# Fewer, larger transfers for wo and w2, an earlier last K, and later zero fills in a decode kernel bound by its loads

## Chip, cores, metric

One core of a Trainium2 chip (trn2). The metric is the device time of one execution in microseconds; a kernel is run several times and the median is given. Ratios are the mean time of one kernel's runs over that of the other's of the same rounds, so they are not quite the ratio of the medians quoted beside them. The limit for "faster" or "slower" is 2%, which is 10.5 us.

## The reference, cut to what matters

Four sequences, one new token each. Attention over the last 2048 positions of a K and V cache (32 heads of 192), its projection with wo, a gated FFN (w1, w3, w2) beside it, and the input added:

```python
B, D, Hq, Dh, Sk, F = 4, 640, 32, 192, 8192, 1536
xn = layernorm(x)                                       # (4, 1, 640) bfloat16
q = xn @ wq                                             # wq (640, 6144)
k, v = k_cache[:, :, Sk - 2048:], v_cache[:, :, Sk - 2048:]
p = softmax(einsum("bhqd,bhkd->bhqk", q, k) * Dh ** -0.5)
attn = einsum("bhqk,bhkd->bhqd", p, v).reshape(4, 1, 6144) @ wo   # wo (6144, 640)
ffn = (silu(xn @ w1) * (xn @ w3)) @ w2                  # w1, w3 (640, 1536), w2 (1536, 640)
return x + attn + ffn
```

K and V of one head are 3072 KB each, 64 such loads; all else together is 21.6 MB. Every byte is used once.

## The kernel before

One stream of loads is issued from the sync engine. A step of the schedule is a quarter of a head: VectorE multiplies K by the query (`mult`), TensorE adds over the head dimension (`adder`), VectorE finishes the scores; then softmax and the products with V (`pv`). Sums of several heads stand in one PSUM bank (`po`) and are scaled, transposed and projected together (`ge_turn`, `ge_proj`).

```python
HG, KBUFS, VBUFS = 4, 2, 3            # four heads per projection group; buffers for K and V
def wo_load(hg):                      # 8 loads, 7680 B in each partition
    wo_t = wopool.tile([P, RPP * D], BF16, tag="wo")                        # RPP = 6, two buffers
    nc.sync.dma_start(out=wo_t[:], in_=A_wo[hg * QW:(hg + 1) * QW, :].rearrange("(p i) n -> p (i n)", i=RPP))
...
qbc = ...                             # the queries, copied from PSUM by ScalarE and VectorE
for i in range(2):                    # zero fills, ahead of the first mult
    o_ps = ps_o.tile([P, 2 * Dh], FP32, tag="o_ps", name="o_ps")
    nc.vector.memset(o_ps[:], 0.0)
acc = ps_acc.tile([P, N0], FP32, name="acc"); nc.vector.memset(acc[:], 0.0)
...
def w1_load():                        # 512 rows, 64 rows as half rows; then the last 64 rows:
    we = wopool.tile([LF, 2 * F], BF16, tag="wo", name="w1e")
    nc.gpsimd.memset(we[:], 0.0); nc.gpsimd.memset(wt[0:LF, FH:], 0.0)
    ...
def w1_low(n):                        # four loads on three DMA engines ("e" is 3)
    nc.sync.dma_start(out=we[n * CT:n * CT + LP, :], in_=w[b0:b0 + 2 * LP, :].rearrange("(i e s) n -> e i (s n)", e=LE, s=2))
    ...
W2C = [0, FC - 8, FC - 4, FC - 1, FC] # w2 in four loads of 4, 4, 3 and 1 rows per partition
...
for h in range(H - 2, H):             # the end: V30, V31, w2, w2, wo, wo, w2, w2
    add(NU - 6, 0, load_v, h)
add(NU - 6, 0, w2_load, 0); add(NU - 6, 0, w2_load, 1)
add(NU - 6, 0, wo_load, NG - 2); add(NU - 6, 0, wo_load, NG - 1)
add(NU - 6, 0, w2_load, 2); add(NU - 6, 0, w2_load, 3)
```

## Time and profile before

| | before |
|---|---|
| time, median of the runs at hand for the prediction | 525.47 us (525.42 to 525.69) |
| span of the profiled execution | 523.7 us |
| bytes read; mean rate | 222.96 MB; 426 GB/s |
| busiest compute engine | PE, 69% of the span |
| DMA packets | 11904 |
| last packet of the load queue ends | 520.63 us |

In the lines of the profile PE is TensorE, PEld its weight loads, DVE VectorE, ACT ScalarE, POOL GpSimd and SPq the queue of the sync engine; "clock" is the share of the full TensorE clock that was granted.

The first thing to see is that all loads together would take 512.3 us on sixteen engines at 27.2 bytes per ns with no fixed cost at all. That leaves little to win anywhere but in the fixed cost of packets, in how evenly the engines are loaded, and in the first and last microseconds. The lines themselves are in the prediction.

### The profile page before, as it was taken

The numbers are of one execution on the slowest core, as the hardware profiler recorded it, in microseconds if no ns is written. First come the engines' busy times: TensorE is split into PE (matmuls) and PEld (weight loads), VectorE is DVE, ScalarE is ACT, GpSimd is POOL, SyncE is SP. The second block draws the span as 40 slices with busy tenths as digits, with TensorE's granted clock in tenths as the row PEclk, the third lists the DMA queues.
The fourth block names the chain that finished last, engine by engine and source line by source line (L and its number), as shares of the span: only waits on it lengthen the run. The fifth ranks groups of instructions, "written<-read, shape, count | busy, mean of one in ns | idle before, by whom it ended". The sixth has DMA issues, their size and how long they took to land.

```text
span 523.7 us, 4813 instructions
## 1 busy us (share of the span) xinstructions
PE 358.9 (69%) x2337; PEld 74.5 (14%) x1643; DVE 339.2 (65%) x410; ACT 57.3 (11%) x179; POOL 5.6 (1%) x12
## 2 busy tenths in 40 slices
PE   0976756887658776757557768576686876655785
PEld 0100111121111111111111111111111111111122
DVE  3248953687656767577647877467666867667671
ACT  2121111111001110110000111001101100001111
POOL 4000000000000000000000000000000000000000
PEclk9989986898788988799987988799878888999889
DMA  9999999999999999999999999999999999999996
GB/s 391 420 443 421 435 431 428 437 427 429 431 435 428 433 424 445 422 434 432 434 432 433 428 435 434 430 429 432 431 435 432 429 435 430 433 432 429 435 422 276
DMA packets 11904, 223.26 MB, mean 426 GB/s; under 512 B 1332, under 2 KB 1608, under 8 KB 3052
## 3 DMA queue, kind: packets, MB, share of 16 engines
q1 hardware_dynamic: 11868, 222.96, 99.3%
q8 instruction: 15, 0.25, 0.2%
q14 instruction: 5, 0.04, 0.0%
q10 hardware_dynamic: 16, 0.01, 0.0%
HBM read 222.96 MB, written 0.01 MB: 426 GB/s over the span
## 4 chain that ended last, share of the span: by engine, by line
DMA 60%; PE 19%; DVE 15%; ACT 3%; issue 2%; SPq 1%; DVEq 0%
DMA kt<-in_A_k_cache_dram 44%; PE ps L303 11%; DMA w<-in_B_w_dram 10%; DVE pr L292 10%; DMA vt<-in_A_v_cache_dram 5%; PE po L376 4%; DVE sc L311 2%; PE qps L258 2%; ACT ex L339 1%; DVE z L347 1%; DMA x_sb<-in_A_x_dram 1%; PE mt L333 1%; ACT L339 0%; ACT negm L336 0%; PE mt L320 0%
## 5 line engine op out<-in xcount | busy, mean ns | idle before, releaser
L303 PE MATMUL ps<-pr,idb 128*128 128x512 bf16 x768 | 217.3, 426 | 140.5 <-DVE pr L292 140.5
L292 DVE TENSOR_TENSOR pr<-kt,qbc 128x3072 bf16<-128x3072 bf16 x128 | 223.5, 1747 | 101.2 <-DMA kt<-in_A_k_cache_dram 101.2
L311 DVE TENSOR_REDUCE sc<-ps 128x16 f32<-128x512 f32 x128 | 87.1, 681 | 2.7 <-PE ps L303 2.7
L355 PE MATMUL o_ps<-vt,z 128*8 128x384 bf16 x1024 | 53.4, 345 | 0.2 <-DVE z L347 0.2
L376 PE MATMUL po<-o_sb,sel_w 128*32 128x192 f32 x128 | 49.2, 518 | 0.6 <-ACT o_sb L358 0.6
L347 DVE TENSOR_TENSOR z<-ex,mask_b 128x256 bf16<-128x256 bf16 x32 | 13.5, 423 | 41.3 <-ACT ex L339 41.3
L355 PEld LDWEIGHTS <-z 128*8 128x8 bf16 x1024 | 24.5, 89 | 95.2 <-issue 83.5
L358 ACT COPY o_sb<-o_ps 128x384 f32<-128x384 f32 x32 | 15.3, 479 | 189.6 <-PE o_ps L355 189.6
L328 ACT ACTIVATE gneg<-gmax 1x128 f32<-1x128 f32 x32 | 9.8, 308 | 164.6 <-DVE gmax L325 164.6
L320 PEld LDWEIGHTS mt<-idf,lmax 128*1 128x1 f32 x32 | 3.4, 105 | 132.1 <-issue 131.1
L376 PEld LDWEIGHTS po<-o_sb,sel_w 128*32 128x32 f32 x128 | 13.9, 131 | 30.0 <-issue 28.8
L303 PEld LDWEIGHTS <-idb 128*128 128x128 bf16 x124 | 12.0, 96 | 37.7 <-issue 31.6
L333 PEld LDWEIGHTS mt<-ones_ff,gneg 1*128 1x128 f32 x64 | 9.6, 186 | 47.9 <-issue 44.5
L258 PE MATMUL qps<-wt,xnT 128*128 128x512 bf16 x60 | 16.2, 438 | 0.0
L336 ACT COPY negm<-mt 128x1 f32<-128x1 f32 x32 | 5.1, 159 | 72.4 <-PE mt L333 72.4
L333 PE MATMUL mt<-ones_ff,gneg 1*128 1x1 f32 x64 | 12.3, 259 | 0.7 <-ACT gneg L328 0.7
L325 DVE TENSOR_REDUCE gmax<-mt 1x4 f32<-1x128 f32 x32 | 8.8, 275 | 6.0 <-PE mt L320 5.7
L363 PEld LDWEIGHTS po<-rsum,tot_w 128*32 128x32 f32 x64 | 4.4, 108 | 51.0 <-ACT ex L339 34.7
L320 PE MATMUL mt<-idf,lmax 128*1 128x128 f32 x32 | 11.3, 353 | 0.0
L339 ACT ACTIVATE ex<-sc,negm 128x64 bf16<-128x64 f32 x32 | 11.1, 348 | 1.0
L279 PE MATMUL acc<-wo_t,oT 128*4 128x320 bf16 x96 | 9.2, 298 | 1.3 <-DMA wo_t<-in_A_wo_dram 1.3
L214 PE MATMUL xnT_ps<-idb,xn 4*128 4x4 bf16 x5 | 0.4, 178 | 13.5 <-DVE xn L209 13.5
(74 smaller groups left out, 78.7 us busy)
## 6 DMA issues: line engine op xcount, KB each, us to landing
kt<-in_A_k_cache_dram SPq DMA_DIRECT2D x32, 3072.0 KB, 19.0
vt<-in_A_v_cache_dram SPq DMA_DIRECT2D x32, 3072.0 KB, 26.1
wo_t<-in_A_wo_dram SPq DMA_DIRECT2D x8, 960.0 KB, 20.8
wt<-in_A_wq_dram SPq DMA_DIRECT2D x2, 3072.0 KB
w<-in_B_w_dram SPq DMA_DIRECT2D x1, 1920.0 KB
wt<-in_A_wq_dram SPq DMA_DIRECT2D x1, 1536.0 KB, 19.5
w<-in_B_w_dram SPq DMA_DIRECT2D x1, 1536.0 KB
w<-in_B_w_dram SPq DMA_DIRECT2D x2, 640.0 KB
```

Of the source, the lines that this page charges most:

```text
L258: nc.tensor.matmul(qp[:], lhsT=xnT[:, kc].rearrange("p a b -> p (a b)"), rhs=wq_rows[kc][:, (c0 + i) * QC:(c0 + i + 1) * QC], start=(kc == ...
L292: nc.vector.tensor_tensor(out=pr[:], in0=kts[h][:, g * JQ:(g + 1) * JQ, :], in1=qbc[:, h * Dh:(h + 1) * Dh].unsqueeze(1).to_broadcast([P, ...
L303: nc.tensor.matmul(ps[:], lhsT=idb[:], rhs=pr[:, :, kk * DD:(kk + 1) * DD], start=(kk == 0), stop=(kk == NK - 1))
L311: nc.vector.tensor_reduce(out=scs[h][:, g * JQ:(g + 1) * JQ], in_=pss.pop(u)[:], axis=AX.X, op=ALU.add)
L320: nc.tensor.transpose(out=mt[0:1, 0:P], in_=chs[h][0][:], identity=idf[:])
L328: nc.scalar.activation(out=gneg[:], in_=gmax[:].unsqueeze(1).to_broadcast([1, PB, B]), func=ACTF.Copy, scale=-SCALE)
L333: nc.tensor.matmul(mt[:, P:P + 1], lhsT=gneg[:].rearrange("o p b -> o (p b)"), rhs=ones_ff[:], start=True, stop=True)
L339: nc.scalar.activation(out=ex[:], in_=scs.pop(h)[:], func=ACTF.Exp, bias=negm[:, 0:1], scale=SCALE, accum_out=rsum[:])
L347: nc.vector.tensor_tensor(out=z[:], in0=ex[:].unsqueeze(2).to_broadcast([P, NJ, B]), in1=mask_b[:].unsqueeze(1).to_broadcast([P, NJ, B]), ...
L355: nc.tensor.matmul(o_ps[c * CT:c * CT + 2 * B, :], lhsT=z[:, 2 * jj:2 * jj + 2, :], rhs=vt[:, 2 * jj:2 * jj + 2, :], start=(jj < 4), stop= ...
L358: nc.scalar.copy(out=o_sb[:], in_=o_ps[:])
L376: nc.tensor.matmul(po[sl, 0:Dh], lhsT=sel_w[:, par].rearrange("p a b -> p (a b)"), rhs=o_sb[:, par * Dh:(par + 1) * Dh].rearrange("p (r i) ...
```

## The change

Its intent: fewer and larger packets (wo by eight heads, w2 at once, w1's last rows in two loads, not four); the last K in ahead of the last three V, so that only V and weights are outstanding at the end; and the first K products no longer behind zero fills that wait for ScalarE. The core of the diff:

```diff
-    HG: int = 4,
+    HG: int = 8,
+    FG: int = 4,
-    wopool = ctx.enter_context(tc.tile_pool(name="wo", bufs=2))
+    wopool = ctx.enter_context(tc.tile_pool(name="wo", bufs=1))
     def load_k(h):
-        kt = kpool.tile([P, NJ, Dh], BF16, tag="kt")
+        kt = (kpool if h < H - 1 else vpool).tile(...)      # load_v: the other way round
...
+    acc = ps_acc.tile([P, N0], FP32, name="acc")            # now before x is there
+    nc.vector.memset(acc[:], 0.0)
...
-    for i in range(2):
-        o_ps = ...; nc.vector.memset(o_ps[:], 0.0)          # ahead of the first mult
+    add(5, 9, o_zero)                                       # the same fills in step 5
...
-        we = wopool.tile([LF, 2 * F], BF16, tag="wo", name="w1e")
-        nc.gpsimd.memset(we[:], 0.0)
-        nc.gpsimd.memset(wt[0:LF, FH:], 0.0)
+        we = wopool.tile([LF, LS, F], BF16, tag="wo", name="w1e")   # LS = 5
+        nc.gpsimd.memset(we[:], 0.0)
...
-    W2C = [0, FC - 8, FC - 4, FC - 1, FC]                   # four w2 loads
+        nc.sync.dma_start(out=wt[:].rearrange("p c n -> p (c n)"), in_=w2_v.rearrange("p c n -> p (c n)"))
-    ends = {H - 2: (NU - 1, NU), H - 1: (NU + 3, NU + 4)}
+    ends = {H - 3: (NU - 1, NU), H - 2: (NU + 2, NU + 3), H - 1: (NU + 4, NU + 5)}
+    early = {H - 1: (NU - 10, -1)}                          # the last K
...
+    WOC = [0, RPP - 5, RPP - 2, RPP]                        # last wo load: 7, 3 and 2 rows
     for h in range(H - 2, H):
         add(NU - 6, 0, load_v, h)
+    add(NU - 6, 0, w2_load)
+    for i0, i1 in zip(WOC, WOC[1:]):
+        add(NU - 6, 0, wo_load, NG - 1, i0, i1)
+        add(e, 6, ge_proj, NG - 1, i0, i1, True)
+    add(e - 1, 8, ffn_out)
```

More of the change, by code (lines that the diff above doesn't have):

```diff
@@ L101 @@
     CT = 32
+    HB = HG * CT // P
     QW = HG * Dh
     RPP = QW // P
+    RW = Dh // RPP
     NU = H * GQ
@@ L109 @@
     assert JQ * DD == 512 and JQ % 2 == 0 and 2 * Dh <= 512 and 2 * N0 == D and N0 <= 512
-    assert (H * Dh) % QC == 0 and NQ % 6 == 0 and QW % P == 0 and Dh == CT * RPP and P == HG * CT and F == HG * CT * FC
-    assert 2 * H * Dh <= NJ * Dh and KBUFS == 2 and VBUFS == 3
+    assert (H * Dh) % QC == 0 and NQ % 6 == 0 and QW % P == 0 and Dh == RW * RPP and CT == HB * RW and P == FG * CT and F == FG * CT * FC
+    assert 2 * H * Dh <= NJ * Dh and KBUFS == 2 and VBUFS == 3 and HB * (Dh + 1) <= 512 and H // HG > 1
     nc.at_finalize(keep_loaded_weights)
@@ L138, in load_k @@
     def load_k(h):
-        kt = kpool.tile([P, NJ, Dh], BF16, tag="kt")
+        kt = (kpool if h < H - 1 else vpool).tile([P, NJ, Dh], BF16, tag="kt" if h < H - 1 else "vt", name="kt")
         nc.sync.dma_start(out=kt[:].rearrange("q j d -> q (j d)"),
@@ L142, in load_k, with load_v, wo_load @@
         kts[h] = kt
-    def load_v(h, n=1):
-        vt = vpool.tile([P, NJ, Dh], BF16, tag="vt")
-        for j in range(0, NJ, NJ // n):
-            nc.sync.dma_start(out=vt[:, j:j + NJ // n].rearrange("q j d -> q (j d)"),
-                              in_=v_win[:, h].rearrange("b (p j) d -> p b j d", p=PB)[:, :, j:j + NJ // n].rearrange("p b j d -> p b (j d)"))
-        vts[h] = vt
-    def wo_load(hg):
-        wo_t = wopool.tile([P, RPP * D], BF16, tag="wo")
-        nc.sync.dma_start(out=wo_t[:], in_=A_wo[hg * QW:(hg + 1) * QW, :].rearrange("(p i) n -> p (i n)", i=RPP))
-        wos[hg] = wo_t
+    def load_v(h):
+        vt = (vpool if h < H - 1 else kpool).tile([P, NJ, Dh], BF16, tag="vt" if h < H - 1 else "kt", name="vt")
+        nc.sync.dma_start(out=vt[:].rearrange("q j d -> q (j d)"),
+                          in_=v_win[:, h].rearrange("b (p j) d -> p b (j d)", p=PB))
+        vts[h] = vt
+    def wo_load(hg, i0=0, i1=RPP):
+        if i0 == 0:
+            wos[hg] = wopool.tile([P, RPP * D], BF16, tag="wo", name="wo_t")
+        nc.sync.dma_start(out=wos[hg][:, i0 * D:i1 * D],
+                          in_=A_wo[hg * QW:(hg + 1) * QW, :].rearrange("(p i) n -> p i n", i=RPP)[:, i0:i1, :].rearrange("p i n -> p (i n)"))
     x_sb = const.tile([B, D], BF16, name="x_sb")
@@ L216 @@
     nc.vector.tensor_copy(out=xnT[:], in_=xnT_ps[:].unsqueeze(2).to_broadcast([P, KC, PB, B]))
-    KM, PH, LE, LI = KC - 1, P // 2, 3, 4
-    LP, LF, LB = LE * LI, CT + LE * LI, KM * P + PH
-    assert D - LB == 5 * LP + LI and F % LE == 0
+    KM, LE, LI, LS = KC - 1, 3, 4, 5
+    LP, LF = LE * LI, CT + LE * LI
+    PH = D - KM * P - LP * LS - LI
+    LB = KM * P + PH
+    assert PH == P // 2 and F % LE == 0
     xm = ppool.tile([B, 2, PH, 2], BF16, tag="pr", name="xm")
@@ L227 @@
         nc.vector.tensor_copy(out=xm[:, i, :, i], in_=xn[:, KM * P:LB])
-    xe = ppool.tile([B, 3 + LE, LF], BF16, tag="pr", name="xe")
+    xe = ppool.tile([B, LS + LE, LF], BF16, tag="pr", name="xe")
     nc.gpsimd.memset(xe[:], 0.0)
-    for g in range(2):
-        b0 = LB + g * 2 * LP
-        nc.vector.tensor_copy(out=xe[:, 0:2, g * CT:g * CT + LP].rearrange("b s (e i) -> b s e i", i=LI),
-                              in_=xn[:, b0:b0 + 2 * LP].rearrange("b (i e s) -> b s e i", e=LE, s=2))
-    nc.vector.tensor_copy(out=xe[:, 2, 0:LP].rearrange("b (e i) -> b e i", i=LI),
-                          in_=xn[:, LB + 4 * LP:LB + 5 * LP].rearrange("b (i e) -> b e i", e=LE))
+    nc.vector.tensor_copy(out=xe[:, 0:LS, CT:LF].rearrange("b s (e i) -> b s e i", i=LI),
+                          in_=xn[:, LB:LB + LS * LP].rearrange("b (i e s) -> b s e i", e=LE, s=LS))
     for e in range(LE):
-        nc.vector.tensor_copy(out=xe[:, 3 + e, CT + e * LI:CT + (e + 1) * LI], in_=xn[:, LB + 5 * LP:D])
-    NX = KM + 2
-    xw_ps = ps_t.tile([P, NX + 3 + LE, B], BF16, tag="t", name="xw_ps")
+        nc.vector.tensor_copy(out=xe[:, LS + e, e * LI:(e + 1) * LI], in_=xn[:, LB + LS * LP:D])
+    xw_ps = ps_t.tile([P, KM + 2 + LS + LE, B], BF16, tag="t", name="xw_ps")
     for kc in range(KM):
@@ L243, with weights @@
         nc.tensor.transpose(out=xw_ps[:, KM + i, :], in_=xm[:, i].rearrange("b r h -> b (r h)"), identity=idb[0:B, 0:B])
-    for i in range(3 + LE):
-        nc.tensor.transpose(out=xw_ps[0:LF, NX + i, :], in_=xe[:, i, :], identity=idb[0:B, 0:B])
-    xw = const.tile([P, NX, NREP, B], BF16, name="xw")
-    nc.vector.tensor_copy(out=xw[:], in_=xw_ps[:, 0:NX, :].unsqueeze(2).to_broadcast([P, NX, NREP, B]))
-    xl = const.tile([LF, 3 + LE, NREP, B], BF16, name="xl")
-    nc.vector.tensor_copy(out=xl[:], in_=xw_ps[0:LF, NX:, :].unsqueeze(2).to_broadcast([LF, 3 + LE, NREP, B]))
+    for i in range(LS + LE):
+        nc.tensor.transpose(out=xw_ps[0:LF, KM + 2 + i, :], in_=xe[:, i, :], identity=idb[0:B, 0:B])
+    def weights(name, p, c0, c1):
+        t = const.tile([p, c1 - c0, NREP, B], BF16, name=name)
+        nc.vector.tensor_copy(out=t[:], in_=xw_ps[0:p, c0:c1, :].unsqueeze(2).to_broadcast([p, c1 - c0, NREP, B]))
+        return t
+    xw = weights("xw", P, 0, KM)
+    xh = weights("xh", P, KM, KM + 2)
+    xl = weights("xl", LF, KM + 2, KM + 2 + LS + LE)
     qbc = const.tile([P, H * Dh], BF16, name="qbc")
@@ L269, with o_zero @@
     o_banks = []
-    for i in range(2):
-        o_ps = ps_o.tile([P, 2 * Dh], FP32, tag="o_ps", name="o_ps")
-        nc.vector.memset(o_ps[:], 0.0)
-        o_banks.append(o_ps)
-    acc = ps_acc.tile([P, N0], FP32, name="acc")
-    nc.vector.memset(acc[:], 0.0)
+    def o_zero():
+        for i in range(2):
+            o_ps = ps_o.tile([P, 2 * Dh], FP32, tag="o_ps", name="o_ps")
+            nc.vector.memset(o_ps[:], 0.0)
+            o_banks.append(o_ps)
     def acc_half(i, lhsT, rhs, first=False, last=False):
@@ L283, in acc_add @@
             acc_half(i, lhsT, rhs, last=last)
-    po = ps_po.tile([P, Dh + 1], FP32, name="po")
+    po = ps_po.tile([P, HB * (Dh + 1)], FP32, name="po")
+    po_v = po[:, 0:HB * Dh].rearrange("p (i x r) -> p i x r", x=HB, r=RW)
     def x_add(i):
@@ L361, in ge_tot @@
     def ge_tot(h):
-        sl = slice((h % HG) * CT, (h % HG + 1) * CT)
-        nc.tensor.matmul(po[sl, Dh:Dh + 1], lhsT=tot_w[:].rearrange("p a b -> p (a b)"), rhs=rsums.pop(h)[:],
-                         start=True, stop=True)
+        blk, x = (h % HG) // HB, h % HB
+        nc.tensor.matmul(po[blk * CT:(blk + 1) * CT, HB * Dh + x:HB * Dh + x + 1], lhsT=tot_w[:].rearrange("p a b -> p (a b)"),
+                         rhs=rsums.pop(h)[:], start=True, stop=True)
         chs.pop(h)
     def ge_rec(hg):
-        rt = small.tile([P, 1], FP32, tag="rt", bufs=2, name="rt")
@@ L369, in ge_rec @@
-        nc.vector.reciprocal(out=rt[:], in_=po[:, Dh:Dh + 1])
+        rt = small.tile([P, HB], FP32, tag="rt", bufs=2, name="rt")
+        nc.vector.reciprocal(out=rt[:], in_=po[:, HB * Dh:HB * (Dh + 1)])
         rts[hg] = rt
     def ge_sum(h):
-        sl = slice((h % HG) * CT, (h % HG + 1) * CT)
+        blk, x = (h % HG) // HB, h % HB
         o_sb = o_sbs.pop(h)
         for par in range(2):
-            nc.tensor.matmul(po[sl, 0:Dh], lhsT=sel_w[:, par].rearrange("p a b -> p (a b)"),
+            nc.tensor.matmul(po_v[blk * CT:(blk + 1) * CT, :, x, :], lhsT=sel_w[:, par].rearrange("p a b -> p (a b)"),
@@ L377, in ge_sum @@
                              rhs=o_sb[:, par * Dh:(par + 1) * Dh].rearrange("p (r i) -> p i r", i=RPP), start=(par == 0), stop=(par == 1))
     def ge_turn(hg):
-        og = small.tile([P, RPP, CT], BF16, tag="og", bufs=1, name="og")
-        nc.vector.tensor_scalar_mul(out=og[:].rearrange("p i r -> p (i r)"), in0=po[:, 0:Dh],
-                                    scalar1=rts.pop(hg)[:, 0:1])
+        og = small.tile([P, RPP, HB, RW], BF16, tag="og", bufs=1, name="og")
+        nc.vector.tensor_tensor(out=og[:], in0=po_v, in1=rts.pop(hg)[:].unsqueeze(1).unsqueeze(3).to_broadcast([P, RPP, HB, RW]),
+                                op=ALU.mult)
@@ L383, in ge_turn, with ge_proj @@
         oT = small.tile([P, RPP, CT], BF16, tag="oT", bufs=2, name="oT")
-        nc.vector.transpose(out=oT[:].rearrange("p i r -> p (i r)"), in_=og[:].rearrange("p i r -> p (i r)"))
+        nc.vector.transpose(out=oT[:].rearrange("p i r -> p (i r)"), in_=og[:].rearrange("p i x r -> p (i x r)"))
         oTs[hg] = oT
-    def ge_proj(hg, i0, i1):
+    def ge_proj(hg, i0, i1, last=False):
         oT, wo_t = oTs[hg], wos[hg]
         for i in range(i0, i1):
-            acc_add(oT[:, i, 0:B], wo_t[:, i * D:(i + 1) * D])
@@ L393 @@
-    FW = F // HG
+            acc_add(oT[:, i, 0:B], wo_t[:, i * D:(i + 1) * D], last=last and i == RPP - 1)
+    FW = F // FG
     sT = const.tile([P, FW], FP32, name="sT")
@@ L397 @@
     ffn = {}
-    FM, FH = KM * F, KM * F + F // 2
+    FM = KM * F
     def w1_load():
-        w = B_w1
-        wt = fpool.tile([P, FH + F], BF16, tag="w", name="w1")
-        we = wopool.tile([LF, 2 * F], BF16, tag="wo", name="w1e")
+        wt = fpool.tile([P, FM + F // 2], BF16, tag="w", name="w1")
+        we = wopool.tile([LF, LS, F], BF16, tag="wo", name="w1e")
         nc.gpsimd.memset(we[:], 0.0)
-        nc.gpsimd.memset(wt[0:LF, FH:], 0.0)
-        nc.sync.dma_start(out=wt[:, 0:FM], in_=w[0:KM * P, :].rearrange("(p kc) n -> p (kc n)", kc=KM))
-        nc.sync.dma_start(out=wt[:, FM:FH], in_=w[KM * P:LB, :].rearrange("r (h n) -> (r h) n", h=2))
+        nc.sync.dma_start(out=wt[:, 0:FM], in_=B_w1[0:KM * P, :].rearrange("(p kc) n -> p (kc n)", kc=KM))
+        nc.sync.dma_start(out=wt[:, FM:], in_=B_w1[KM * P:LB, :].rearrange("r (h n) -> (r h) n", h=2))
         ffn["w1"], ffn["w1e"] = wt, we
     def w1_low(n):
-        w, wt, we = B_w1, ffn["w1"], ffn["w1e"]
-        if n < 2:
-            b0 = LB + n * 2 * LP
-            nc.sync.dma_start(out=we[n * CT:n * CT + LP, :],
-                              in_=w[b0:b0 + 2 * LP, :].rearrange("(i e s) n -> e i (s n)", e=LE, s=2))
-        elif n == 2:
-            nc.sync.dma_start(out=wt[0:LP, FH:FH + F], in_=w[LB + 4 * LP:LB + 5 * LP, :].rearrange("(i e) n -> e i n", e=LE))
+        b0, we = LB + LS * LP, ffn["w1e"]
+        if n == 0:
+            nc.sync.dma_start(out=we[CT:LF].rearrange("p s n -> p (s n)"),
+                              in_=B_w1[LB:b0, :].rearrange("(i e s) n -> e i (s n)", e=LE, s=LS))
         else:
-            nc.sync.dma_start(out=wt[CT:LF, FH:FH + F // LE], in_=w[LB + 5 * LP:D, :].rearrange("i (e n) -> e i n", e=LE))
+            nc.sync.dma_start(out=we[0:LP, 0, 0:F // LE], in_=B_w1[b0:D, :].rearrange("i (e n) -> e i n", e=LE))
     def w1_in():
@@ L426, in mm @@
         def mm(w, lhsT, rhs, c0=0, start=False, stop=False):
-            nc.tensor.matmul(ps[w * CT:(w + 1) * CT, c0:c0 + rhs.shape[1]], lhsT=lhsT.rearrange("p a b -> p (a b)"), rhs=rhs,
-                             start=start, stop=stop)
+            nc.tensor.matmul(ps[w * CT:(w + 1) * CT, c0:c0 + rhs.shape[1]], lhsT=lhsT.rearrange("p a b -> p (a b)"), rhs=rhs, start=start, stop=stop)
         def main(kc):
-            for w in range(HG):
+            for w in range(FG):
                 mm(w, xw[:, kc], wt[:, kc * F + w * FW:kc * F + (w + 1) * FW], start=(kc == 0), stop=(kc == KM - 1))
         main(0)
-        for w in range(HG):
+        for w in range(FG):
             c0 = FM + (w % 2) * FW
-            mm(w, xw[:, KM + w // 2], wt[:, c0:c0 + FW])
-        for i in range(2):
-            for w in range(HG):
-                mm(w, xl[:, i], we[:, i * F + w * FW:i * F + (w + 1) * FW])
-        for w in range(HG):
-            mm(w, xl[:, 2], wt[0:LF, FH + w * FW:FH + (w + 1) * FW])
+            mm(w, xh[:, w // 2], wt[:, c0:c0 + FW])
+        for i in range(LS):
+            for w in range(FG):
+                mm(w, xl[:, i], we[:, i, w * FW:(w + 1) * FW])
         FE = F // LE
         for e in range(LE):
-            for w in range(HG):
+            for w in range(FG):
                 c0, c1 = max(e * FE, w * FW), min((e + 1) * FE, (w + 1) * FW)
                 if c0 < c1:
-                    mm(w, xl[:, 3 + e], wt[0:LF, FH + c0 - e * FE:FH + c1 - e * FE], c0 - w * FW)
+                    mm(w, xl[:, LS + e], we[:, 0, c0 - e * FE:c1 - e * FE], c0 - w * FW)
         for kc in range(1, KM):
@@ L459, in w3_in @@
         for kc in range(KC):
-            for w in range(HG):
+            for w in range(FG):
                 nc.tensor.matmul(ffn["ps"][w * CT:(w + 1) * CT, :], lhsT=xnT[:, kc].rearrange("p a b -> p (a b)")[:, 0:CT],
@@ L473, with w2_load, ffn_out @@
     w2_v = B_w2.rearrange("(p c) n -> p c n", c=FC)
-    W2C = [0, FC - 8, FC - 4, FC - 1, FC]
-    def w2_load(i):
-        if i == 0:
-            ffn["w2"] = fpool.tile([P, FC, D], BF16, tag="w", name="w2")
-        c0, c1 = W2C[i:i + 2]
-        nc.sync.dma_start(out=ffn["w2"][:, c0:c1, :].rearrange("p c n -> p (c n)"),
-                          in_=w2_v[:, c0:c1, :].rearrange("p c n -> p (c n)"))
-    def ffn_out(i):
-        for c in range(*W2C[i:i + 2]):
-            acc_add(hT[:, c, 0:B], ffn["w2"][:, c, :], last=(c == FC - 1))
+    def w2_load():
+        wt = fpool.tile([P, FC, D], BF16, tag="w", name="w2")
+        nc.sync.dma_start(out=wt[:].rearrange("p c n -> p (c n)"), in_=w2_v.rearrange("p c n -> p (c n)"))
+        ffn["w2"] = wt
+    def ffn_out():
+        for c in range(FC):
+            acc_add(hT[:, c, 0:B], ffn["w2"][:, c, :])
     sched = defaultdict(list)
@@ L497 @@
         if h >= KBUFS:
-            add((h - KBUFS + 1) * GQ, 0, load_k, h)
+            add(*early.get(h, ((h - KBUFS + 1) * GQ, 0)), load_k, h)
         if h < H - 2:
@@ L518 @@
     e = ends[H - 1][1] + 1
-    for hg in range(NG - 2):
+    for hg in range(NG - 1):
         a = ((hg + 1) * HG - 1) * GQ + L + 3
-        add(hg * HG * GQ + 8, 0, wo_load, hg)
-        add(a, 6, ge_proj, hg, 0, RPP // 2)
-        add(a + 1, 6, ge_proj, hg, RPP // 2, RPP)
+        add(hg * HG * GQ + 17, 0, wo_load, hg)
+        for n in range(4):
+            add(a + n, 6, ge_proj, hg, n * RPP // 4, (n + 1) * RPP // 4)
+    add(5, 9, o_zero)
     add(3, 0, w1_load)
-    for n in range(4):
-        add(4 + 2 * n, 1, w1_low, n)
+    for n in range(2):
+        add(5 + 3 * n, 1, w1_low, n)
     add(13, 7, w1_in)
@@ L533 @@
     add(17, 6, x_add, 1)
+    WOC = [0, RPP - 5, RPP - 2, RPP]
     for h in range(H - 2, H):
         add(NU - 6, 0, load_v, h)
-    add(NU - 6, 0, w2_load, 0)
-    add(NU - 6, 0, w2_load, 1)
-    add(NU - 6, 0, wo_load, NG - 2)
-    add(NU - 6, 0, wo_load, NG - 1)
-    add(NU - 6, 0, w2_load, 2)
-    add(NU - 6, 0, w2_load, 3)
-    add(e - 1, 8, ffn_out, 0)
-    add(e - 1, 8, ffn_out, 1)
-    add(e - 1, 8, ge_proj, NG - 2, 0, RPP)
-    add(e, 6, ge_proj, NG - 1, 0, RPP)
-    add(e, 7, ffn_out, 2)
-    add(e, 7, ffn_out, 3)
+    add(NU - 6, 0, w2_load)
[3 more added lines that the diff above has]
+    add(e - 1, 8, ffn_out)
     for s in sorted(sched):
```

## The prediction

> **What bounds the kernel now.** I read the page first (parts 1 to 3), then a table of stretches, then the waits of the load queue, then the last microseconds and the first 36 in order of time, and last the trace's packet records. The page:
>
> ```profile
> PE 358.9 (69%) x2337; PEld 74.5 (14%) x1643; DVE 339.2 (65%) x410; ACT 57.3 (11%) x179; POOL 5.6 (1%) x12
> ...
> DMA  9999999999999999999999999999999999999996
> ...
> HBM read 222.96 MB, written 0.01 MB: 426 GB/s over the span
> ```
>
> No compute engine is busy for more than 69% of the 523.7 us span, and the transfers are at 90% or more in 39 of 40 slices. The stretches (us, PE, PEld, DVE, ACT, POOL, clock, DMA share, GB/s):
>
> ```profile
> 10.00:500.00 490.00, 341.95 (x2182) 68.33 (x1506) 325.86 (x383) 51.71 (x165) 3.09 (x2) 0.89 1.01 432
> 500.00:516.00 16.00, 13.18 (x107) 3.96 (x91) 8.97 (x13) 2.77 (x10) 0.00 (x0) 0.92 0.99 419
> 516.00:521.00 5.00, 3.53 (x52) 2.13 (x52) 0.80 (x2) 0.00 (x0) 0.00 (x0) 1.00 0.68 279
> 521.00:524.00 3.00, 0.25 (x4) 0.03 (x1) 0.48 (x1) 0.42 (x1) 0.00 (x0) 0.82 0.01 2
> ```
>
> The DMA share is 1.01 over 490 us: all 16 engines move data without a gap. Only the last five microseconds fall off (0.68). The load queue waits a lot,
>
> ```profile
> SPq L140 <- DVE pr L292: 316.1, 30, 13.1
> ```
>
> (316.1 us in all, 30 times, 13.1 the longest), but it waits with two or more 3072 KB loads still queued (a K load takes 19.0 us from issue to landing; one such load takes 7.3 us of the engines), so the wait costs nothing. The chain of waits, which gives 44% to K loads and 11% to a PE line, must be read in that light: its PE and DVE pieces lie beside running transfers.
>
> The packet records say what sets the end. One engine takes 908 ns from packet to packet for 24576 B, 569 for 15360 B, 287 for 7680 B, 193 for 5120 B, 146 for 3840 B, 52 for 1280 B. From the first and the third, a packet costs 4.75 ns plus its bytes at 27.2 bytes per ns; the 4-byte record that closes a transfer costs 5.9 ns. The last packets end between 517.3 us (the earliest engine) and 520.63 us (the last). The mean idle time of the 16 engines before 520.63 is 1.14 us. I can follow engines in the records: three carry the last 64 rows of w1 alone (65.5 KB each, 2.4 us); seven others each carry two of the 15 instruction packets of 16384 B, and each of these delays its engine by 1.4 us. These ten end near 520.2, the most delayed at 520.63; engines with neither end near 517.5. The end after that:
>
> ```profile
> 519.38 0.98 PE L279 MATMUL acc<-wo_t,oT 128*4 128x320 bf16 x12 [1.29 <-DMA wo_t<-in_A_wo_dram]
> ...
> 520.54 0.71 PE L279 MATMUL acc<-w,hT 128*4 128x320 bf16 x8 [0.18 <-DMA w<-in_B_w_dram]
> ...
> 521.29 0.48 DVE L557 CAST res<-acc 4x320 bf16<-4x320 f32 x1 [2.93 <-PE acc L279]
> ```
>
> The projection waits for wo, the last products for w2: compute is ahead of data by 1.29 us even at the end. From the last packet to the end of the span are 523.74 - 520.63 = 3.1 us. So span = 1.0 us start + 519.6 us of the most loaded engine + 3.1 us.
>
> **What the Trainium skill says.** "DMA: Bandwidth & Descriptors", section "Where 436 GB/s comes from", gives 435.2 GB/s for 16 ports; 16 times 27.2 here is 435.2, and the trace agrees. The same page, "Why small descriptors are slow", describes a fixed cost per packet; here it is 4.75 ns, 1.6% of a 7680 B packet and 0.5% of a 24576 B one. Its section "Why a DMA increments its semaphore by 16 and not by 1" has the number of engines follow from the slowest dimension of both sides: a transfer whose source starts with a dimension of 3 lies on three engines, which is what the records show for the last w1 rows. "SBUF — State Buffer", "Who interferes with whom", says that a GpSimd operation and a two-port VectorE operation lock each other out for the whole instruction. The first microseconds agree:
>
> ```profile
> 8.26 0.54 DVE L198 TENSOR_SCALAR xc<-xf,negmean 4x640 f32<-4x640 f32 x1
> ...
> 11.39 2.04 DVE L209 TENSOR_SCALAR xn<-xc,rstd 4x640 bf16<-4x640 f32 x1
> ```
>
> The second took 2.04 us beside two GpSimd memsets (9.12 to 11.77 and 11.72 to 13.09) and ended 0.34 us after them.
>
> **The change part by part.** The 222.96 MB stay the same, so only packets, balance, start and tail can move.
>
> *Packets.* wo: 8 transfers of 8 packets per engine (64 of 7680 B) become 3 of 8 (15360 B) and one in three pieces (8960, 3840, 2560 B): 48, so 16 fewer. w2: 4 times 8 becomes 8, 24 fewer. 40 x 4.75 = 0.19 us per engine. Closing records: 12 become 7, 5 x 5.9 = 0.03 us. Together 0.22 us on every engine, all on the path. On the three w1 engines, 16 packets and 4 closings become 8 and 2: 0.05 us more. Their 65.5 KB stay, and the balance is untouched.
>
> *Instruction packets.* w1 now has five packed slices, not three: 8 products more, and two more transposes. With their weight loads some 20 PE instructions on 4022. A packet came every 255 or so and the 15th at PE instruction 3832; the 16th would come near 4088, beyond 4042. No change; a 16th would fall on the engine with only one, which has 2 us to spare.
>
> *Start.* The zero fills of the two sum banks stood at 32.13 us, waiting for ScalarE to empty those banks, ahead of the first K product at 33.24 us. Behind five products they let it begin once the first query columns are copied (24 us) and K0 has landed (about 26.5); the adders then wait only for the query matmuls, at 31.5 instead of 35.0: 3.6 us earlier. Against it: w1's padded tile is now one memset of 7680 columns; at 2.65 us for 3072 it takes 6.6 us, from 9.12 to 15.8. The normalised x then ends near 16.1 instead of 13.43, and all query matmuls move back 2.7 us. Net the first adders come 0.9 us earlier. The K2 load goes out near 41.5 instead of 42.47. V0 goes out near 30.3 instead of 27.6, while the queue holds work to 33.8 us (14.2 MB at 435 GB/s plus 1.3). Neither runs dry. Worth 0.
>
> *Middle.* The last w1 piece is no longer queued behind wo and V2; the 3.7 us for which PE waited for it, beside running transfers, go. Four head groups instead of eight halve the turn operations. Worth 0.
>
> *Tail.* The last K, one V place earlier, is in by about 490 us instead of 497. V31 lands near 511.3. After it 4.6 (w2) + 2.7 + 1.2 + 0.8 us of wo follow. Its products (1.47), copy (0.48), head sums (1.5), scaling and transpose (0.42 + 0.38 doubled) are done near 517, before the first wo piece (518.8). So the last wo piece decides: its packets end 0.22 us earlier than w2's did. But two rows hang on it, not one: 4 products instead of 2, one pair more at 0.135 us. Net 0.09 us.
>
> The sum: -0.22 + 0.13 = -0.09 us certain. A little more is likely, as 520.63 was the worst of ten engines that otherwise ended near 520.2, and the next draw is likelier to be lower: I take another -0.13. 525.47 - 0.22 = 525.25 us.
>
> **Rivals.** (1) The queue runs dry near 33 us, because the longer memset delays V0's buffer. Against: 3 us of margin by the sum above, less about 1 from issue to first packet. If the margin is misjudged by 2 us it costs up to 1: 526.2. (2) The end becomes compute: eight heads in one group put a whole wo half behind one turn (scaling from PSUM with a broadcast, on twice the columns). Against: 1.3 us of slack before, more with K early; if it failed, 526. (3) The balance changes: if instruction packets spread otherwise or the three w1 engines are relieved, up to the mean idle of 1.14 us could be had: 524.3. Nothing in the diff touches it. (4) Earlier compute shortens the kernel, as the chain's shares suggest (PE 19%, DVE 15%): 3 us or more. Against: a DMA share of 1.01.
>
> **Range and chances.** Three runs before lay within 0.27 us. With 0.3 us either way for the worst engine and a small chance each of rivals 1 to 3, 524.7 to 525.8 should hold it 8 times in 10. Two per cent are 10.5 us: no rival but a broken pipeline reaches that. Faster 0.007, same 0.985, slower 0.008.
>
> **What would show it.** Right: HBM bytes unchanged, DMA share of 1.0 from 10 to 516 us, packets down by about 750 (40 x 16, 24 for w1, some 80 closings), 15 instruction packets, first K product near 27 us, the normalised x near 16, the last products waiting for wo, four of them after its landing, span near 523.5. Wrong: a slice below 0.95 near 33 or 45 us (rival 1), the last proj released by DVE (rival 2), last packets of all engines within 1 us of each other (rival 3).

## The result

525.66 us (525.46 to 525.88, 6 runs) against 525.46 us (525.41 to 525.69, 6 runs) for the kernel before; ratio 1.0003 with a 95% interval of 0.999 to 1.0016. The time is the same. It lies inside the predicted range, 0.4 us above the predicted value. A second comparison of the same two kernels (first experiment) gave 525.61 against 525.62.

The page of the kernel after, the lines that answer to those of before:

```profile
PE 349.5 (67%) x2346; PEld 74.9 (14%) x1652; DVE 340.5 (65%) x397; ACT 57.3 (11%) x179; POOL 8.2 (2%) x11
...
DMA  9999999999999999999999999999999999999996
...
DMA packets 11155, 223.27 MB, mean 427 GB/s; under 512 B 1246, under 2 KB 1394, under 8 KB 1650
...
q8 instruction: 16, 0.26, 0.2%
...
HBM read 222.96 MB, written 0.01 MB: 426 GB/s over the span
```

749 packets fewer, the same bytes, the same 426 GB/s. The stretches (us, PE, PEld, DVE, ACT, POOL, clock, DMA share, GB/s) show where nothing changed and where a little did:

```profile
10.00:500.00 490.00, 333.31 (x2171) 68.49 (x1488) 330.20 (x373) 52.30 (x169) 6.19 (x1) 0.91 1.01 432
500.00:516.00 16.00, 12.39 (x129) 4.48 (x120) 6.44 (x12) 2.64 (x9) 0.00 (x0) 1.00 0.98 420
516.00:521.00 5.00, 3.80 (x48) 1.94 (x44) 0.11 (x2) 0.04 (x1) 0.00 (x0) 1.00 0.63 256
```

From 10 to 500 us the engines of the queue are full, as before (1.01, 432 GB/s). The last stretch is emptier (0.63 for 0.68): the queue is done earlier. By the packet records its last packet ends at 520.16 us; before it was 520.63. Now the first microseconds of the kernel after, in order of time:

```profile
9.71 6.49 POOL L413 MEMSET w1e<- 44x7680 bf16 x1
...
11.91 4.63 DVE L215 TENSOR_SCALAR xn<-xc,rstd 4x640 bf16<-4x640 f32 x1
...
28.56 3.42 DVE L301 TENSOR_TENSOR pr<-kt,qbc 128x3072 bf16<-128x3072 bf16 x2
...
30.39 0.54 SPq L149 DMA_DIRECT2D vt<-in_A_v_cache_dram  x1
...
40.23 0.54 SPq L143 DMA_DIRECT2D kt<-in_A_k_cache_dram  x1
```

In the kernel before, the first products stood behind the fills:

```profile
32.13 0.87 DVE L272 MEMSET o_ps<- 128x384 f32 x2 [6.28 <-ACT qbc L266]
...
33.24 3.40 DVE L292 TENSOR_TENSOR pr<-kt,qbc 128x3072 bf16<-128x3072 bf16 x2
```

The normalised x ends at 16.54 us instead of 13.43, held up by the longer fill (0.5 us of it is that x itself was taken up later in this profile, at 7.24 instead of 6.72 us); the first K products start at 28.56 instead of 33.24; V0 (line 149) is issued at 30.39 instead of 27.60, and K2 (line 143) at 40.23 instead of 42.47. And the last microseconds:

```profile
515.46 0.58 DVE L393 STREAM_TRANSPOSE oT<-og 128x384 bf16<-128x384 bf16 x1
515.88 1.79 PE L287 MATMUL acc<-w,hT 128*4 128x320 bf16 x24 [1.05 <-DMA w<-in_B_w_dram]
...
518.55 1.71 PE L287 MATMUL acc<-wo_t,oT 128*4 128x320 bf16 x20 [0.87 <-DMA wo_t<-in_A_wo_dram]
...
520.46 0.44 PE L287 MATMUL acc<-wo_t,oT 128*4 128x320 bf16 x4 [0.20 <-DMA wo_t<-in_A_wo_dram]
...
520.93 0.48 DVE L551 CAST res<-acc 4x320 bf16<-4x320 f32 x1 [4.89 <-PE acc L287]
```

The turned heads are ready at 516.04 us, 2.5 us before the first wo piece; before, they were ready at 518.36 us, 1.0 us ahead of wo:

```profile
517.98 0.38 DVE L384 STREAM_TRANSPOSE oT<-og 128x192 bf16<-128x192 bf16 x1
```

All three groups of products still wait for a load. From the last packet to the end of the span it is 3.32 us; before it was 3.11.

Following engines through the packet records of the kernel after shows who ends when (one engine could not be followed without doubt):

| engines | last packet ends |
|---|---|
| with neither extra load nor 16384 B instruction packets (4) | 517.0 to 517.8 us |
| with one such instruction packet in the traced stretch (1) | 518.6 |
| three that carry the last w1 rows | 519.6 to 520.1 |
| one with three 8192 B instruction packets | 519.6 |
| with two 16384 B instruction packets | 519.8 to 520.16 |

### The profile page after: what moved, and what is told of

Its sections match the earlier page's. It is cut to its first block, busy times and chain, and to the rows that moved or that the text cites. A ratio compares the mean times of both kernels' runs of the same rounds, so it can differ in the third digit from the quotient of the medians.

```text
span 523.5 us, 4807 instructions
## 1 busy us (share of the span) xinstructions
PE 349.5 (67%) x2346; PEld 74.9 (14%) x1652; DVE 340.5 (65%) x397; ACT 57.3 (11%) x179; POOL 8.2 (2%) x11
## 4 chain that ended last, share of the span: by engine, by line
DMA 61%; DVE 19%; PE 17%; ACT 2%; issue 1%; SPq 0%
DMA kt<-in_A_k_cache_dram 52%; DVE pr L301 12%; PE ps L312 8%; DMA wo_t<-in_A_wo_dram 7%; PE po L385 3%; PE qps L266 3%; DVE sc L320 3%; DMA x_sb<-in_A_x_dram 1%; DVE z L356 1%; ACT ex L348 1%; DVE xn L215 1%; PE mt L342 1%; PE f_ps L431 1%; ACT negm L345 0%; PE mt L329 0%
## 5 line engine op out<-in xcount | busy, mean ns | idle before, releaser
L312 PE MATMUL ps<-pr,idb 128*128 128x512 bf16 x768 | 207.2, 410 | 148.7 <-DVE pr L301 148.7
L364 PE MATMUL o_ps<-vt,z 128*8 128x384 bf16 x1024 | 51.7, 342 | 0.9 <-DMA vt<-in_A_v_cache_dram 0.9
```

Of the source, the lines that this page charges most:

```text
L312: nc.tensor.matmul(ps[:], lhsT=idb[:], rhs=pr[:, :, kk * DD:(kk + 1) * DD], start=(kk == 0), stop=(kk == NK - 1))
L364: nc.tensor.matmul(o_ps[c * CT:c * CT + 2 * B, :], lhsT=z[:, 2 * jj:2 * jj + 2, :], rhs=vt[:, 2 * jj:2 * jj + 2, :], start=(jj < 4), stop= ...
```

## The experiments

Twelve kernels were run. The first is the kernel after without an edit, the tenth has two edits, all others have one. They ran in three sets: 1, 2, 3 and 5; then 7, 8, 9 and 11; then 4, 6, 10 and 12. The kernel before ran beside each set and gave 525.62, 525.66 and 525.69 us. The kernel after ran in the first set alone (525.61, and 525.66 in the result above); in the other two the kernel before, which it equals, stands in for it wherever the text says "longer" or "shorter".

### 1. The changed kernel again

No edit.

> The changed kernel unchanged, timed again beside the kernel before, to see whether the 0.2 us between the two medians (525.66 against 525.46) is real. My sum said 0.09 us faster for certain, 0.22 with a lucky worst engine. If the sum holds and the first comparison was scatter: the difference of the means between -0.25 and +0.1 us. If something that the sum left out was added (rival: about +0.3 us outside the sum, such as one instruction packet more or work outside the span): +0.1 to +0.3 us again.

Measured: 525.61 us (5 runs) against 525.62 (9 runs of the kernel before); ratio 0.9999, interval 0.9986 to 1.0013. The difference of the means is -0.02 us, after +0.17 us in the first comparison. So the first difference was scatter for the greater part, and the runs can't tell my -0.09 us from zero. They do speak against my -0.22.

The record also holds the span of nearly every run, to 0.1 us. Eleven runs of the kernel after have a mean of 523.60 us, 25 of the kernel before 523.73: 0.13 us less, with a standard error of 0.045 (in the rounds of this experiment alone 0.12, error 0.08). What the device time has beyond the span is 2.04 us against 1.96, 0.09 more with an error of 0.05. So from the first instruction to the last the kernel did become shorter by about what was predicted, and the device time seems to have lost it outside the span. What lies there is not on record, and the second difference is hardly out of the noise.

### 2. A useless load on three engines, in one portion

```diff
+    more = const.tile([72, 2 * D], BF16, name="more")
+        nc.sync.dma_start(out=more[:], in_=A_wo[0:144, :].rearrange("(i e s) n -> e i (s n)", e=3, s=2))
+    add(60, 0, more_load)
```

> A useless load of 184 KB is added whose source starts with a dimension of 3, so that it should lie on three engines, 24 packets of 2560 B on each: 24 x 98.9 ns = 2.37 us on these three. Theory (the most loaded engine sets the end, and these three end within 0.1 us of the last one): 2.2 to 2.4 us longer than the changed kernel, 527.9 us. Rival (the engines share the work, the mean counts): 2.37 x 3 / 16 = 0.45 us longer, 526.1 us.

Measured: 529.39 us, ratio 1.0069 to the kernel before: 3.7 us longer, more than either. The packet records divide it. From 521.4 to 523 us only three engines still move data, until 523.95 us: the mean doesn't count, the most loaded engine does. But beside the useless load, from 273 to 278 us, packets of 24576 B took 1000 to 1670 ns on all sixteen engines instead of 912, so that the thirteen others also end about 1.1 us later (at 521.3 us). The rest, 2.6 us, is the predicted 2.37 and a little.

### 3. Nearly the same bytes on sixteen engines

```diff
+    more = const.tile([P, F // 2], BF16, name="more")
+        nc.sync.dma_start(out=more[:], in_=B_w1[0:P // 2, :].rearrange("r (h n) -> (r h) n", h=2))
+    add(60, 0, more_load)
```

> A useless load of 197 KB over all sixteen engines, 8 packets of 1536 B on each: 8 x 61 + 6 = 0.49 us on every engine. Both theories say 0.5 us longer than the changed kernel, 526.15 us. It is the control of the run before it: nearly the same bytes, another spread.

Measured: 526.17 us, 0.54 us more than the kernel before of the same rounds, which the kernel after equals there. Predicted 0.5. The packet times hold, and 197 KB spread out cost a seventh of what 184 KB on three engines cost.

### 4. The portion on three engines cut into three

```diff
+    more = const.tile([24, 2 * D], BF16, name="more")
+        nc.sync.dma_start(out=more[:], in_=A_wo[n * 48:(n + 1) * 48, :].rearrange("(i e s) n -> e i (s n)", e=3, s=2))
+    for n in range(3):
+        add(45 + 24 * n, 0, more_load, n)
```

> The useless load on three engines in three portions of 61 KB far apart in time, 8 packets of 2560 B on each of the three engines: again 24 x 98.9 = 2.37 us on these. In the run with one portion all sixteen engines lost some 1.1 us beside it. Theory (three engines set the end by what is put on them, and the loss of all engines came from so much in one burst): 2.2 to 2.6 us longer than the changed kernel, 528.0 us. Rival (every such packet delays the other engines too): 3.5 us or more, as before.

Measured: 528.65 us (528.38 to 529.93), ratio 1.006: 2.96 us by the medians over the kernel before, with one run 1.1 us above the next; that is between the 2.6 us of the theory and the 3.5 us of its rival. In the profiled execution the last packet ends at 522.73 us, 2.57 us later than in the kernel after. The other engines are delayed beside each portion here too: 46 packets of 24576 B took over 960 ns (at most 1274), beside 47 (at most 1673) with the one portion. What they lose over 912 ns each sums to 6.2 us here and to 17.5 us there, by sixteen engines 0.4 and 1.1 us, and the thirteen others end later than in the kernel after by just that (520.57 and 521.30 against 520.16 us). So the loss of all engines shrinks to about a third with small portions and doesn't vanish. With the predicted 2.37 us of the three engines on top this makes 2.75 us here and 3.5 us there; measured on the last packet were 2.57 and 3.79 us. The three engines' share is thus confirmed within 0.3 us in both. Why a burst on three engines slows all sixteen is not settled.

### 5. Rows of wo and w2 apart

```diff
-            wos[hg] = wopool.tile([P, RPP * D], BF16, tag="wo", name="wo_t")
+            wos[hg] = wopool.tile([P, RPP, D + 16], BF16, tag="wo", name="wo_t")
-        wt = fpool.tile([P, FC, D], BF16, tag="w", name="w2")
+        wt = fpool.tile([P, FC, D + 16], BF16, tag="w", name="w2")
```

(and the loads and products that go with it)

> wo and w2 in the same transfers as the changed kernel, but each row of 1280 B lands 32 B apart from the next, so that every row must be a packet of its own. Per engine: 3 wo loads x 88 more packets, the last wo load 96 instead of 24, w2 96 instead of 8: 424 packets more, at 4.75 ns = 2.0 us. Theory (a packet costs 4.75 ns of its engine, and the engines set the end): 2.0 us longer than the changed kernel, 527.7 us. Rival (the fixed cost hides in other work, for packets follow one another without waiting): under 0.5 us longer.

Measured: 531.55 us, 5.9 us longer, three times what I expected. The edit did more than I meant. By the packet records one engine now takes 55 ns, not 52, from packet to packet for 1280 B, and 912.6 ns, not 908.9 (an eighth of the time from one closing record to the next), for the untouched 24576 B of K and V, whose buffers lie 32 B times some rows further on than before. 480 x 3 and 528 x 3.7 ns are 3.4 us; with the 2.0 us for 424 packets that makes 5.4 of the 5.8 us by which the last packet ends later. The Trainium skill ("DMA: Bandwidth & Descriptors", "How a descriptor splits into AXI transactions") says that a descriptor which doesn't start at a multiple of 256 B costs further beats; that fits, but no run here moved an address alone.

### 6. K and V in two halves each

```diff
-        nc.sync.dma_start(out=kt[:].rearrange("q j d -> q (j d)"), in_=k_win[:, h]....rearrange(..."p b (j d)"))
+        for j in range(0, NJ, NJ // 2):                    # and the same for V
+            nc.sync.dma_start(out=kt[:, j:j + NJ // 2].rearrange("q j d -> q (j d)"), in_=...[:, :, j:j + NJ // 2]...)
```

> Every K and V is loaded in two transfers of 12288 B per partition instead of one of 24576 B; the addresses keep their alignment, unlike in the run with rows apart. Per engine 64 x 8 = 512 packets and 64 closing records more: 512 x 4.75 + 64 x 5.9 ns = 2.8 us. Theory (a packet costs 4.75 ns of its engine, and what the run with rows apart took beyond that came from its addresses): 2.6 to 3.0 us longer than the changed kernel, 528.4 us, as long as the queue doesn't run dry. Rival (the cost of one packet more is 13 to 14 ns, which is what 5.9 us over 424 packets would be): 7.5 us longer, 533 us.

Measured: 529.99 us, ratio 1.008: 4.3 us over the kernel before. The rival's 7.5 us are out, but my 2.8 us are too low for the time. For the packets they are right: from one closing record to the next it is 3657.6 ns here for most transfers (8 packets of 12288 B), twice which is 43.5 ns more than the 7271.7 ns of 8 packets of 24576 B in the kernel after; that is 8 x 4.7 ns and one closing record more, and 64 times 43.5 ns are 2.8 us. In the profiled execution the last packet ends 3.6 us later than in the kernel after (523.73 us). Most of the 0.8 us between the two are packets that took longer than is usual for their size: together they lose 1.84 us per engine here and 1.25 in the kernel after; why is not settled. Another 0.8 us lie behind the last packet (4.17 us to the end of the span instead of 3.32). The stretches and the tail of this run:

```profile
520.00:524.00 4.00, 4.00 (x34) 2.01 (x32) 0.00 (x0) 0.00 (x0) 0.00 (x0) 0.50 0.65 263
...
519.47 3.36 PE L289 MATMUL acc<-w,hT 128*4 128x320 bf16 x24 [1.06 <-DMA w<-in_B_w_dram]
...
522.62 2.69 PE L289 MATMUL acc<-wo_t,oT 128*4 128x320 bf16 x24
...
525.35 0.48 DVE L553 CAST res<-acc 4x320 bf16<-4x320 f32 x1 [5.73 <-PE acc L289]
```

The granted clock is 0.50 here, and the 24 products of w2 took 3.36 us where the kernel after needs 1.79 at a clock of 1.00. With that the products, not the loads, set the end: all 24 products of wo run on without a wait for a load. In this one execution rival 2 of the prediction came true, through the clock.

### 7. The w1 fill early

```diff
+    we = wopool.tile([LF, LS, F], BF16, tag="wo", name="w1e")
+    nc.gpsimd.memset(we[:], 0.0)                            # now ahead of the two small fills
     xm = ppool.tile([B, 2, PH, 2], BF16, tag="pr", name="xm")
```

(and gone from `w1_load`)

> The zero fill of the padded w1 tile is put ahead of the other GpSimd fills, into the time in which everything waits for x. The normalised x should then end near 13 us instead of 16.54 and the query matmuls start 3 us or more earlier. Theory (compute is ahead of the transfers from the first microseconds on, and 3 us more of lead are worth nothing): the time within 0.15 us of the changed kernel, 525.6 us. Rival (the changed kernel lost at the start what it won at the end): 0.3 us or more faster, 525.3 us or less.

Measured: 525.66 us against 525.66 of the kernel before; the normalised x takes 0.54 us and ends at 14.16 us, and K2 goes out at 37.20 us, 3.0 us earlier than in the kernel after. (It is 14.16 and not 13, for the early fill now holds small VectorE copies ahead of x for 6 us, so that x is taken up at 8.96 us instead of 7.24.) Three microseconds of lead, nothing won, as the theory had it.

### 8. The w1 fill twice

```diff
         nc.gpsimd.memset(we[:], 0.0)
+        nc.gpsimd.memset(we[:], 0.0)
```

> The padded w1 tile is filled with zeros twice: 6.5 us more on GpSimd, and the normalised x, the query matmuls and the buffer that V0 waits for should come 6.5 us later, V0 issued near 36.9 us with its first packet near 37.9, while the queue holds work to 33.8. Theory: 4 us of idle engines near 34 us and the time longer by 3.5 to 4.5 us, 529.6 us. Rival (my reading of 3 us of margin is wrong by a lot in either direction): unchanged, or longer by the whole 6.5 us.

Measured: 527.98 us, ratio 1.0044: 2.3 us longer. V0 goes out at 35.38 us (not 36.9, for the query matmuls came 5.4 us later, not 6.5). Here the expectation was wrong about the path: the normalised x ended at 16.20 us as before, between the two fills, and it was the small copies behind it that waited for the second one (until 22.65 us):

```profile
17.06 5.67 DVE L235 COPY xm<-xn 4x64 bf16<-4x64 bf16 x2
```

The stretches show the queue dry:

```profile
32.00:34.00 2.00, 1.99 (x9) 0.19 (x2) 2.00 (x4) 1.08 (x3) 0.00 (x0) 1.00 1.03 442
34.00:36.00 2.00, 1.95 (x10) 0.10 (x1) 2.00 (x2) 0.00 (x0) 0.00 (x0) 1.00 0.03 12
36.00:38.00 2.00, 2.00 (x11) 0.20 (x2) 0.96 (x1) 0.00 (x0) 0.00 (x0) 1.00 0.72 197
```

The share falls to 0.03 for two microseconds, and by the packet records the engines idle 38.3 us together, 2.4 us each: the whole loss, and nothing of it was made up later. This also measures the margin: V0 came 5.33 us later than in the kernel after (30.05 us in the second profile of it) and lost 2.4, so 2.9 us are free (2.6 us from the first profile, where all came 0.4 us later). The prediction had taken 3 less about 1.

### 9. The zero fills of the sum banks first

```diff
-    add(5, 9, o_zero)
+    o_zero()                                                # ahead of all steps
```

> The zero fills of the two sum banks go back ahead of the first K product, everything else as changed. The first product then waits for ScalarE again, which with the longer w1 fill is at 36.1 us, and the K2 load goes out near 45.2 us instead of 40.2. The queue holds work to 45.2 us by the packet times (33.8 + V0 7.3 + w1 3.65 + 0.49), and the first packet comes about 1 us after the issue. Theory (the lead has a limit, and this move was what paid for the longer fill): the engines idle for about 1 us near 45 us and the time grows by 0.6 to 1.4 us, to 526.6 us. Rival (all of it is hidden): within 0.15 us of the changed kernel.

Measured: 526.61 us, ratio 1.0016 (interval 1.0002 to 1.0031): 0.9 us longer. K2 goes out at 44.49 us. The fills wait as in the kernel before, and the product behind them:

```profile
34.49 0.87 DVE L282 MEMSET o_ps<- 128x384 f32 x2 [6.28 <-ACT qbc L274]
35.27 3.40 DVE L301 TENSOR_TENSOR pr<-kt,qbc 128x3072 bf16<-128x3072 bf16 x2
```

From 45.9 to 48 us most engines have one packet of 24576 B at 1000 to 1500 ns or a gap of some 0.5 us, and the last packet of all ends at 521.30 us, 1.1 us later than in the kernel after; the other fifteen engines end by 520.72 us, some 0.6 us later. So this part of the change is worth 0.9 us (0.4 to 1.3 by the four runs), in the presence of the longer fill.

### 10. Fills first, and the w1 fill early

The edits of 7 and 9 together.

> The zero fills of the sum banks ahead of the first K product, as in the run that lost 1 us, but with the w1 fill in the early place. The K2 load should go out near 42 us. Theory (the move of the fills is worth something only because the w1 fill has become longer): within 0.15 us of the changed kernel, 525.6 us. Rival (the fills cost by themselves): about 526.6 us, as in the run before.

Measured: 525.80 us, 0.1 us above the kernel before (525.69), ratio 1.0002. The loss of experiment 9 is gone for the most part. Moving the fills buys nothing by itself that the runs could show (525.66 us with it in experiment 7); it pays for the longer w1 fill that the same change brought in.

### 11. The last K late

```diff
-    ends = {H - 3: (NU - 1, NU), H - 2: (NU + 2, NU + 3), H - 1: (NU + 4, NU + 5)}
-    early = {H - 1: (NU - 10, -1)}
+    ends = {H - 2: (NU - 1, NU), H - 1: (NU + 3, NU + 4)}
+    early = {}
```

(and K and V in their own pools)

> The last K back in its old place, behind one V more, with the old steps for the last two heads; all else as changed. Its scores are then ready some 7 us later (near 513.4 us as in the kernel before), the turn of the last eight heads near 518.6 us, about when the first wo piece lands. Theory (the last wo piece decides, and the early K buys only slack): within 0.15 us of the changed kernel, 525.6 us. Rival (with eight heads in one group the turn is on the path): 0.3 to 1 us longer.

Measured: 525.70 us against 525.66, ratio 1.0. The tail shows how close it is:

```profile
517.63 0.58 DVE L393 STREAM_TRANSPOSE oT<-og 128x384 bf16<-128x384 bf16 x1
518.27 0.08 PEld L287 LDWEIGHTS <-oT 128*4 128x4 bf16 x1 [0.85 <-DVE oT L393]
518.64 1.70 PE L287 MATMUL acc<-wo_t,oT 128*4 128x320 bf16 x20 [0.88 <-DMA wo_t<-in_A_wo_dram]
```

The turned heads come at 518.21 us and the wo piece lets the products start at 518.64: 0.43 us of slack, where the kernel after has 2.5. The early K is worth slack, not time.

### 12. A last piece of one row

```diff
-    WOC = [0, RPP - 5, RPP - 2, RPP]
+    WOC = [0, RPP - 6, RPP - 3, RPP - 1, RPP]
```

> The last wo load in pieces of 6, 3, 2 and 1 rows instead of 7, 3 and 2, so that only two products hang on the last landing. One pair less is 0.135 us off the end, one piece more is 8 x 4.75 + 6 = 0.044 us: 0.09 us faster than the changed kernel, about 525.5 us. The scatter of the runs is larger; what can be seen is the tail of its profile: from the last landing to the last product 0.3 us instead of 0.44. Rival: the many small packets at the end stretch, and nothing is won.

Measured: 525.68 us (5 runs) against 525.69, ratio 1.0: no difference that the runs could show. In its profile the result is taken up 0.65 us after the last packet (520.86 against 520.21 us), in the kernel after 0.77 (520.93 against 520.16). That is the expected 0.12 us or so of the pair. But from the last packet to the end of the span it is still 3.29 us (3.32 in the kernel after): at the end the sync engine has one wait more, at 522.77 us ahead of two at 522.84 and 522.90. No version here beats both kernels.

## Why the prediction was right, point by point

- **The bound.** Right, and shown: the queue's engines are full from 10 us on (1.01), and what is put on three of them lengthens the kernel (experiments 2 and 4), while 3 us of compute lead are worth nothing (7).
- **Packets, -0.22 us.** 749 packets fewer, as counted ("about 750"). What a packet costs is confirmed: 4.75 ns from the records of the kernel before, 4.7 ns in experiment 6. In device time the gain of 0.22 us was not seen; the shorter spans (experiment 1) agree with it.
- **Instruction packets.** Wrong: I wrote that the count stays at 15. It was 16; the last came at 519.72 us, when only the last wo piece was outstanding. The profiles of experiments 7 and 12 have 15. I had taken an even interval of 255 instructions, but the trace of the kernel before has 203 to 303 between one packet and the next. The reason given for its harmlessness, that it would fall on an engine with time to spare, was not tested.
- **Start.** The lock between the GpSimd fill and the normalised x, and its size, were right (16.1 predicted, 16.54 measured, and 16.14 in the second profile, where x came 0.4 us earlier; V0 at 30.3 and 30.39). The first product came at 28.56 us, not 27: VectorE first had to finish its own three query copies. K2 went out at 40.23, not 41.5: twelve adder matmuls took 2.75 us instead of 4.33, in a stretch with a clock of 1.00, where the kernel before was granted 0.50 to 0.71. All of it is off the path, as said; experiment 8 gives the margin (2.9 us) that I had only added up.
- **Middle, 0.** Right: 1.01 and 432 GB/s in both.
- **Tail, +0.13 us.** The mechanism was right (four products behind the last landing). The term was too small: from the last packet to the end it is 3.32 us instead of 3.11, +0.21. Some 0.12 us are the pair of products. Another 0.06 us stands in the trace behind the output's landing: two waits of the sync engine at 522.83 and 522.89 us, where the kernel before had one (523.15). I had not looked at the end of the program.
- **The lucky draw, -0.13 us.** Open. Device time did not show it: two comparisons of medians gave +0.20 and -0.01 us. The profiles fit it: the last packet ends at 520.16 to 520.25 us in the five of the kernel after and of the edits that change nothing (1, 7, 11, 12), some 0.4 to 0.5 us before the 520.63 of the single one of the kernel before, where packets and draw together should give 0.35. But with one profile of the kernel before, its draw can't be told from its packets. A term as large as the scatter should have widened the range and not moved the value.
- **The sum.** -0.22 and the tail's +0.21 alone make -0.01 us; with the draw it is -0.14, which is near the 0.13 us by which the mean span became shorter, and then some 0.09 us were lost outside the span. Both fit a device time that stays the same; the spans favour the second. Either way the mis-sized term is the end after the last packet, and that the value came within 0.4 us owes as much to the smallness of all terms as to the sum.
- **Rivals.** 1 (dry queue) did not happen, but it lies 2.9 us away and costs one for one (8). 2 (compute at the end) did not happen in the kernel after; it happened in one execution of experiment 6 with the clock at 0.50. 3 (balance) is untouched: the engines still end between 517.0 and 520.16 us. 4 is refuted by experiment 7.

So where did the intended gain go? 0.2 us of packets are real, but most of it is spent on one more pair of products and one more wait at the end, and perhaps 0.09 us outside the span; the early K and the moved fills act on work that is hidden. The moved fills in addition make good 0.9 us that the same change would have lost through its longer w1 fill.

## What to carry to other kernels

When the load queue is full throughout, count the time of its most loaded engine, from its packets, and the stretch after its last packet; all else is slack, and slack should be measured as a margin (make the suspected thing later until the time moves). A change that moves fixed costs of nanoseconds must be weighed against every term of the same size, the last waits of the program included. A part of a change that seems to do nothing may be paying for another: undo parts one by one and also two at a time.

## What the Trainium skill lacked or had wrong

- "DMA: Bandwidth & Descriptors", "Why small descriptors are slow": gives a fixed overhead of some 3 cycles per packet and treats it as a matter of small ones. Here it was 4.7 ns for packets up to 24576 B, and at a full queue that is time: 512 packets and 64 closing records more per engine took 2.8 us of each.
- "Runtime: NRT & Kernel Launch", "Instruction fetch mechanics": has instructions fetched by DMA in blocks of 16 KiB, one for 256 instructions, which agrees (16384 B every 203 to 303 TensorE instructions in the kernel before). It calls the cost mostly hidden. Lacking: what a block costs a full load queue. Each held one engine for 1.4 us (922 ns for the block and 1406 ns for the load's next packet of 24576 B, instead of 912), seven engines twice in the kernel before.
- "DMA: Bandwidth & Descriptors", "Why a DMA increments its semaphore by 16 and not by 1": the choice of three engines for a leading dimension of 3 agrees. Lacking: 24 packets of 2560 B on each of three engines in one burst slowed packets of 24576 B on all sixteen from 912 to as much as 1670 ns for some 4 us, a loss of 1.1 us per engine; in three portions of 8 packets the loss was 0.4 us per engine.
- "SBUF — State Buffer", "Who interferes with whom": the lock agrees (0.54 us alone, 4.63 us beside the fill). Lacking: in the kernel before, the VectorE operation began its wait during one GpSimd fill (until 11.77 us) and ended after the next one too (13.09 us), so it waited for two instructions in a row; but in experiment 8 it ended at 16.20 us, between a fill until 15.86 and one from 15.92. What decides is not settled.
